# Other columns for the accumulators of a weighted sum, in a kernel that runs a state-space layer and a local attention side by side

## The chip, the cores and the metric

The kernel runs on one core of a Trainium2 chip. The metric is the device time of one execution in microseconds (us). Before the change the median of three executions is 146.32 us (145.62 to 147.16).

## The reference

Two independent layers read two inputs x of 2048 positions by 448 channels (bf16), and their results are laid side by side. Part A is a diagonal complex recurrence with 448 states, part B is attention with 16 heads of 28 channels, in which each position looks at itself and at seven earlier positions, two apart.

```python
# A: h[t] = Lam_bar * h[t-1] + B_bar x[t];  y = 2 Re(C h) + x * Dskip
Bu = jnp.einsum("bld,pd->blp", x + 0j, B_bar)
for t in range(L):
    h = Lam_bar[None, :] * h + Bu[:, t, :]
y = 2.0 * jnp.einsum("blp,dp->bld", hseq, Cmat).real + x * Dskip[None, None, :]
# B: H = 16, Dh = 28, W = 8, dil = 2
qkv = (x @ wqkv) ...            # q, k, v of (H, S, Dh)
idx = pos[:, None] - off[None, :]          # off = 0, 2, ..., 14
logits = jnp.einsum("bhsd,bhswd->bhsw", q, kg) * scale    # kg, vg gathered by idx
attn = _softmax(logits, axis=-1)           # masked where idx < 0
o = jnp.einsum("bhsw,bhswd->bhsd", attn, vg)
out_B = o.reshape(B, S, D) @ wo
return jnp.concatenate([y, out_B], axis=-1)
```

## The kernel before

A position is 16 p + j: the partition p (128 of them) counts blocks of 16 positions, and j (0 to 15) counts inside a block. The neighbours of a position in part B then mostly lie in the same partition at another j; those that fall into the block before are copied there, one partition down. These copies of v are the "halo": its rows 0 to 13 in the tile `vd` stand ahead of the 16 rows of v itself. `halo` (L746) issues two transfers (L749, L750) for each of four groups of rows.

Part B works in this order. TensorE projects q and k (`qk_ps`, L472 to L505) and v (`v_ps`, L735); ScalarE and VectorE evict them from PSUM. VectorE multiplies q and k (L639, L643), TensorE adds the products up by head into `logits` (L654, L660). `softmax` runs for two halves of j, b = 1 (j from 8) and b = 0: a maximum on VectorE (L677, L679), its subtraction on TensorE (L683), the exponential on ScalarE (L689), the sum on TensorE (`sm_ps`, L694), the reciprocal and the product on VectorE (L698, L700), transposes on TensorE (`pt_at`, L706) and a copy by ScalarE (L711). Then `pv` forms the weighted sum of v on VectorE: for each of four groups g = 3, 2, 1, 0 of four rows j, four products of 3584 columns (L791), three additions (L794) and one last addition that folds the two halves of the accumulator (L803; for g = 0 TensorE adds the halves, L806 and L843). The first product of a group is written straight into the accumulator. A DMA transpose (L831) turns the folded accumulators of g = 3, 2, 1 for the last projection (`wo_ps`, L860), ScalarE evicts that (L866) and SyncE's queue sends it out (L869).

Part A multiplies x by B (`scP`, `scb`, L1181 and L1189), runs the recurrence as a scan of doubling steps for seven groups m of states on TensorE (L1198 to L1258) with a ScalarE eviction after each step, and ends with y = C h (`y_ps`, L1345, and the skip term), evicted by ScalarE (L1354) or VectorE (L1356) and sent out by L1359. VectorE also builds the tables of powers `pw` (L1135).

Memory is re-used. The tile `rb` (13568 columns, tag "RB") holds the weights of q and k in columns 0 to 3583, those of v in 3584 to 5375 and x in 5376 to 13567. When q and k are projected, `load_c` loads C over the first weights: eight transfers (L958) into `cn2`, columns 0 to 3583 of `rb`, and one DMA transpose of these (L962) into the tile `Ccat`, which y = C h reads. After that `pv` asks the pool for a second tile with the same tag, `rb2`, which takes the place of `rb`; the accumulators lie in it. In the same way `vd` (tag "RA") takes the place of the tile `ra`, which held the raw x of part B for j from 12 (`x3`, columns 0 to 1855) and the raw B of part A (`bX`, columns 7168 to 10751, read by L1119). `late` (tag "RC") takes the place of q and k. The pool's framework, not the kernel, puts the semaphores in, from the accesses that it sees in program order.

The order of the work is written out by hand. Every piece of work is a unit of a `Planner`, numbered in the order of its `P.add`, with an engine, a cost, dependences and a priority. If `ORDER` has as many entries as there are units (604), as here, the sorted order is replaced by it:

```python
        if len(ORDER) == n:
            for i in ORDER:
                u = self.units[i % 1000]
                u.on = u.eng[i // 1000]
                order.append((0.0, u, 0.0))
            order = order[n:]
        for _, u, _ in order:
            if len(u.eng) > 1:
                u.fn(u.on)
            else:
                u.fn()
```

An entry from 1000 on gives a unit that two engines can do to the second of them (VectorE instead of ScalarE). The units that matter here:

| unit | what | line |
|---|---|---|
| 481, 482, 483, 484 | the four halo groups, SP, two transfers each | L749, L750 |
| 154 | loads of C into `rb`, SP, eight transfers | L958 |
| 155 | transpose of C into `Ccat`, SP | L962 |
| 171, 172 | loads of wo, SP, eight transfers, and their copies to the other partitions, two | L394, L399, L400 |
| 561, 562 | row of Dskip into `rb2`, and x of part A into `late`, SP | L1309, L1318 |
| 485 to 488 | weighted sum of g = 3, VectorE | L791 to L803 |
| 213, 215, 216, 217 | second softmax (b = 0): subtraction, sum, reciprocal with product, transposes | L683, L694, L698, L706 |
| 493, 494, 528 | transposes of the folded accumulators g = 3, 2, 1, SP | L831 |
| 601, 597, 603 | last three outputs of A, SP | L1359 |
| 538, 543, 548, 533 | last four outputs of B (j = 1, 2, 3, 0), SP | L869 |

SP, ScalarE, VectorE, GpSimd and TensorE each run their units in the order of `ORDER`; a unit that waits holds up those behind it on its engine.

Of the kernel before, what the change touches and what calls it, by code (L numbers as in the profile page):

```python
# [10 lines left out]
ALU = mybir.AluOpType  # L11
# [7 lines left out]
NCH = 128  # L19
# [21 lines left out]
FILL = (1, 3)  # L41
PRI = dict(bm=-5.66, xa=2.77, cc=19.9, sc=2.9, ch=-27.35, bk=-0.56, v0=16.0, v1=-26.16, wo=-13.74, y=14.16, pw=-5.68, sm=13.48, lim=100.0, lim2=30.0, limv=70.0, qk=0.86, K11=-14.0, Q11=-13.0, K10=-12.0, Q10=-11.0, K01=-10.0, Q01=-9.0, K00=-8.0, Q00=-7.0, d3=10.94, h0=-1.0, g0=-1.0, h1=-1.0, g1=-1.0, h2=-1.0, g2=-1.0, h3=1.0, g3=-1.0, h4=-1.0, g4=-1.0, h5=-1.0, g5=-1.0, h6=1.0, g6=1.0, nd=4.0, xd=20.12)
ORDER = [
# [28 lines left out]
TWO_PI = 2.0 * math.pi  # L72
MAGIC = 12582912.0

# [234 lines left out]
class PartB:  # L309
# [411 lines left out]
    def v_proj(self, prio, deps):  # L721
        nc, pool, P, cx = self.nc, self.pool, self.plan, self.cx
        self.u_v, self.u_vh, self.u_vm = {}, {}, []

        def va():
            if not hasattr(self, "vd"):
                t = pool.tile([NCH, TJ * D], bf16, name="vd", tag="RA")
                self.vd = t[:].rearrange("p (j d h) -> p j d h", d=DH, h=H)
        for n, j in enumerate((8, 9, 10, 11, 12, 13, 14, 15, 7, 6, 5, 4, 3, 2, 1, 0)):
            box = {}  # L730

            def mm(j=j, box=box):
                ps = box["ps"] = self.psum.tile([NCH, H, DH], f32, name="v_ps", tag="s")
                for k in range(KT):
                    nc.tensor.matmul(ps[:].rearrange("p h d -> p (h d)"), lhsT=self.xT[:, j, k, :],  # L735
                                     rhs=self.wv[:, k, :], start=(k == 0), stop=(k == KT - 1))

            def ev(eng, j=j, box=box):
                va()
                cx.copy(eng, self.vd[:, HALO + j], box["ps"][:].rearrange("p h d -> p d h"))  # L740
            u = P.add("PE", pe(4, 448), mm, [self.u_x[j], self.u_w[2], *deps],
                      prio[n // 8], acq="s")
            self.u_vm.append(u)
            self.u_v[j] = cx.evict(448, ev, [u, *deps], prio[n // 8], rel="s", until=PRI["limv"])

        def halo(i0, i1):  # L746
            f = lambda a, b, p0, p1: self.vd[p0:p1, a:b].rearrange("p j d h -> p (j d h)")
            s0, s1 = i0 + T, i1 + T
            nc.sync.dma_start(f(i0, i1, 1, 113), f(s0, s1, 0, 112))  # L749
            nc.sync.dma_start(f(i0, i1, 113, 128), f(s0, s1, 112, 127))  # L750

        def zero():
            va()
            nc.gpsimd.memset(self.vd[0:1, 0:HALO].rearrange("p j d h -> p (j d h)"), 0.0)
        z = P.add("POOL", 6.0, zero, deps, prio[0])
        for i0, i1 in ((10, 14), (6, 10), (2, 6), (0, 2)):
            h = P.add("SP", 0.2, lambda i0=i0, i1=i1: halo(i0, i1), [self.u_v[i + 2] for i in range(i0, i1)],
                      prio[1], lat=4.0)
            for i in range(i0, i1):
                self.u_vh[i] = [h, z]  # L760

    def pv(self, b, prio, deps):
# [3 lines left out]
        def alloc():  # L766
            if not hasattr(self, "rb2"):
                self.rb2 = pool.tile([NCH, 13568], bf16, name="rb2", tag="RB")
                self.acc = {}
                for i, g in enumerate((3, 2, 1, 0)):  # L770
                    self.acc[g] = self.rb2[:, 1792 * i:1792 * i + 3584]
                self.oT = self.rb2[:, 10752:12288].rearrange("p (r k c) -> p r k c", r=3, k=KT)
                self.oT_ring = Ring(3)
        n1 = 4 * D
        lasts = {}
        for r in (1, 0):
            last = getattr(self, "pv_last", None)
            us = (5, 4, 1, 0)
            for n in range(4):

                def step(n=n, r=r, part=0):
# [13 lines left out]
                    if n == 0:  # L795
                        mul(0)
                        mul(1)
                    elif n < 3:
                        mul(n + 1)
                        add(n)  # L800
                    elif 2 * b + r > 0:
                        add(3)
                        V.tensor_tensor(acc[:, 0:n1], acc[:, 0:n1], acc[:, n1:2 * n1], op=ALU.add)  # L803
                    else:
                        a, t = (v.rearrange("p (y j c) -> p y j c", y=2, j=4)[:, :, 2 * part:2 * part + 2] for v in (acc, tmp[3]))
                        V.tensor_tensor(a, a, t, op=ALU.add)  # L806
# [17 lines left out]
        for r in (1, 0):  # L824
            g = 2 * b + r
            if g > 0:

                def trd(g=g):
                    o = (0, 1792, 0, 8960)[g]
                    t = self.oTd[g] = self.rb2[:, o:o + n1].rearrange("p (k q) -> p k q", q=NCH)  # L830
                    nc.sync.dma_start(t, self.acc[g][:, 0:n1], transpose=True)  # L831
                trs[r] = P.add("SP", 2.5, trd, [lasts[r][1]], PRI["wo"], lat=2.0)
        for j in range(j0, j0 + JB):
            jb = {}
# [2 lines left out]
            def tr(j=j, jb=jb):  # L837
                pt = jb["pt"] = self.psum.tile([NCH, KT, NCH], f32, name="pt_o", tag="s")
                a = j % 4 * D
                for kt in range(KT):  # L840
                    for y in range(2):
                        c = 5376 + y * n1 + a + kt * NCH
                        nc.tensor.matmul(pt[:, kt, :], lhsT=self.rb2[:, c:c + NCH], rhs=cx.ident[:],  # L843
                                         start=(kt == 0 and y == 0), stop=(y == 1), skip_group_check=True)

# [540 lines left out]
def kernel(  # L1386
# [51 lines left out]
    b.softmax(0, 2.6)  # L1438
    a.scan(PRI["sc"], b.u_prod[0] + b.u_prod[1])
    b.v_proj((PRI["v0"], PRI["v1"]), a.u_bm)  # L1440
    b.pv(1, 4, a.u_cc)
    b.pv(0, 5, [])
    a.load_skip([b.u_first])
    a.outputs(PRI["y"])
    plan.run()
# [30 lines left out]
```

## Time and profile before

| | |
|---|---|
| median of three executions | 146.32 us (145.62 to 147.16) |
| the profiled execution | 147.02 us |
| its span, first to last instruction | 145.3 us |
| TensorE busy | 136.7 us (94%) |
| VectorE busy | 122.7 us (84%) |
| ScalarE busy | 91.5 us (63%) |
| mean granted clock of TensorE | 0.986 |
| all DMA traffic | 15.99 MB, mean 110 GB/s |

Times in the views are microseconds from the first instruction. PE is TensorE's matmuls, DVE VectorE, ACT ScalarE, POOL GpSimd, SP SyncE, and SPq its queue of DMA issues. A name like `L791` is a line of the kernel, `rb<-attn,vd` what is written and read; numbers behind tile names are left out, so `rb` also stands for `rb2`. The granted clock is the share of TensorE's full speed that it was given.

### The profile page before, as it was taken

To read this page: it belongs to the slowest core of one execution; us is meant where nothing else is said; L and a number is where in the kernel's file an instruction comes from. 1 tells how busy PE (TensorE), PEld (TensorE's weight loads), DVE (VectorE), ACT (ScalarE), POOL (GpSimd) and SP (SyncE) were. 2 spreads that over 40 slices of the span, in tenths; PEclk is the share of its full clock that TensorE was granted. 3 is DMA by queue.
4 is the path that set the end of the run, shared out by engine and by line. 5 is a ranking of instruction groups with operands and counts; after the bars stand their busy time and mean duration, and the time that the engine had idled before them with its cause. 6 is when DMAs were issued, how large, how long until landed. Compare 5 with 4: busy or idle time off the path is not lost.

```text
span 145.3 us, 2812 instructions
## 1 busy us (share of the span) xinstructions
PE 136.7 (94%) x1078; PEld 72.1 (50%) x1078; DVE 122.7 (84%) x132; ACT 91.5 (63%) x179; POOL 24.8 (17%) x68
## 2 busy tenths in 40 slices
PE   5999999999999999999997599999999999999990
PEld 1633433456464455675363246445565555555660
DVE  3357899999989899893299999999999999999740
ACT  3336969999775964667886239867984434224181
POOL 7382399901920000000000000000000000000000
PEclk9999999999999999999999959999999999999999
DMA  4955434995347448989452000640019252734034
GB/s 132 258 110 106 81 70 82 264 191 62 81 85 71 94 123 176 164 245 196 101 120 58 0 0 5 122 131 0 34 45 162 87 184 82 170 99 145 13 122 131
DMA packets 39390, 15.99 MB, mean 110 GB/s; under 512 B 31445, under 2 KB 38740, under 8 KB 39377
## 3 DMA queue, kind: packets, MB, share of 16 engines
q1 hardware_dynamic: 39314, 15.82, 50.0%
q8 instruction: 8, 0.13, 0.4%
q14 instruction: 5, 0.04, 0.1%
q10 hardware_dynamic: 63, 0.01, 0.0%
HBM read 4.27 MB, written 3.67 MB: 55 GB/s over the span
## 4 chain that ended last, share of the span: by engine, by line
PE 71%; ACT 10%; DVE 7%; DMA 5%; POOL 2%; issue 2%; SPq 1%; POOLq 0%; DVEq 0%; ACTq 0%
PE y_ps L1345 15%; PE wo_ps L860 8%; PE qk_ps L472 7%; PE v_ps L735 7%; DMA Ccat<-rb 5%; PE scb L1181 5%; PE scP L1181 5%; ACT qk L204 3%; ACT qk L202 3%; DVE prods L791 3%; PE logits L654 3%; PE scb L1198 2%; PE y_ps L1342 2%; PE scb L1223 2%; PE qk_ps L479 1%
## 5 line engine op out<-in xcount | busy, mean ns | idle before, releaser
L639 DVE TENSOR_TENSOR prods<-qk 128x3072 bf16<-128x3072 bf16 (+1 forms) x18 | 24.8, 1412 | 1.0 <-PE logits L654 0.6
L791 DVE TENSOR_TENSOR prods<-attn,vd 128x3584 bf16<-128x3584 bf16 x12 | 24.0, 2018 | 0.0
L794 DVE TENSOR_TENSOR rb<-rb,prods 128x3584 bf16<-128x3584 bf16 x11 | 22.2, 2020 | 0.1
L1218 ACT CAST pbuf<-scb 128x128 bf16<-128x128 f32 x35 | 9.3, 279 | 9.0 <-PE scb L1223 7.5
L472 PE MATMUL qk_ps<-rb 128*128 128x512 bf16 x60 | 14.9, 385 | 0.0
L1345 PE MATMUL y_ps<-Ccat,late 128*128 128x448 bf16 x64 | 14.9, 352 | 0.0
L860 PE MATMUL wo_ps<-wo_p,rb 128*128 128x448 bf16 x64 | 13.7, 352 | 0.0
L735 PE MATMUL v_ps<-rb 128*128 128x448 bf16 x64 | 13.3, 353 | 0.0
L1354 ACT CAST late<-y_ps 128x896 bf16<-128x896 f32 x6 | 5.4, 905 | 11.4 <-PE y_ps L1345 11.4
L791 DVE TENSOR_TENSOR rb<-attn,vd 128x3584 bf16<-128x3584 bf16 x4 | 8.1, 2023 | 4.9 <-DMA Ccat<-rb 4.8
L1181 PE MATMUL scb<-xaT_sb,Bcat 128*128 128x512 bf16 x42 | 11.7, 398 | 0.0
L1345 PE MATMUL y_ps<-Ccat,h 128*128 128x448 bf16 x48 | 11.7, 353 | 0.0
L1181 PEld LDWEIGHTS <-Bcat 128*128 128x128 bf16 x84 | 7.6, 99 | 7.8 <-issue 2.4
L1181 PE MATMUL scP<-xaT_sb,Bcat 128*128 128x512 bf16 x42 | 11.2, 379 | 0.0
L202 ACT CAST qk<-qk_ps 128x512 bf16<-128x512 f32 (+2 forms) x13 | 7.4, 582 | 4.7 <-PE qk_ps L472 3.2
L866 ACT CAST late<-wo_ps 128x448 bf16<-128x448 f32 x16 | 8.2, 540 | 3.3 <-PE wo_ps L860 2.8
L202 ACT CAST vd<-v_ps 128x448 bf16<-128x448 f32 x16 | 8.0, 542 | 2.8 <-PE v_ps L735 2.7
L1223 PEld LDWEIGHTS <-pw 128*128 128x128 bf16 x70 | 5.8, 101 | 7.6 <-issue 4.5
L472 PEld LDWEIGHTS <-rb 128*128 128x128 bf16 x60 | 5.8, 100 | 7.1 <-issue 1.2
L1345 PEld LDWEIGHTS <-late 128*128 128x128 bf16 x64 | 6.3, 98 | 5.8
L643 DVE TENSOR_TENSOR prods<-qk 128x768 bf16<-128x768 bf16 (+3 forms) x18 | 9.1, 566 | 0.0
L204 ACT ACTIVATE qk<-qk_ps 128x512 bf16<-128x512 f32 (+1 forms) x15 | 8.5, 603 | 0.2 <-PE qk_ps L505 0.2
(177 smaller groups left out, 256.8 us busy)
## 6 DMA issues: line engine op xcount, KB each, us to landing
out_dram<-late SPq DMA_DIRECT2D x18, 112.0 KB, 1.7
out_dram<-late SPq DMA_DIRECT2D x7, 224.0 KB, 2.3
vd<-vd SPq DMA_DIRECT2D x3, 392.0 KB, 4.2
rb<-in_B_wqkv_dram SPq DMA_DIRECT2D x3, 336.0 KB, 4.5
late<-in_A_x_dram SPq DMA_DIRECT2D x1, 448.0 KB, 4.1
ra<-in_A_B_re_dram SPq DMA_DIRECT2D x1, 392.0 KB, 4.4
ra<-in_A_B_im_dram SPq DMA_DIRECT2D x1, 392.0 KB
rb<-in_A_C_re_dram SPq DMA_DIRECT2D x4, 98.0 KB, 3.0
```

What stands on the lines that cost most here:

```text
L202: nc.scalar.copy(out, in_)
L204: nc.scalar.mul(out, in_, scale)
L472: nc.tensor.matmul(out(n), lhsT=w(n, full, k), rhs=self.xT[:, j:j + 4, k, :], start=(not rfirst and k == 1), stop=(rfirst and k == KT - 1) ...
L639: V.tensor_tensor(out.rearrange("p i j k q -> p i (j k) q"), qq.unsqueeze(1).to_broadcast([NCH, 2, 4 * nk, NCH]), bass.AP(kk.tensor, kk.of ...
L643: V.tensor_tensor(jk(out[:, i, a:e]), qq, kk, op=ALU.mult)
L735: nc.tensor.matmul(ps[:].rearrange("p h d -> p (h d)"), lhsT=self.xT[:, j, k, :], rhs=self.wv[:, k, :], start=(k == 0), stop=(k == KT - 1))
L791: V.tensor_tensor(tmp[i].rearrange("p (j d h) -> p j d h", j=8, d=DH), aa, self.vd[:, o:o + 8], op=ALU.mult)
L794: V.tensor_tensor(acc, acc, tmp[i], op=ALU.add)
L860: nc.tensor.matmul(ps[:], lhsT=o[:, kt, :], rhs=self.wo_p[:, KT * e + kt, :], start=(kt == 0), stop=(kt == KT - 1))
L1181: mt(box[i], lhsT=self.Bcat[:, k, m, :], rhs=self.xk(slice(i, None, 4), k), start=(i % 2 == 0 and k == 0), stop=False, **kw)
L1218: nc.scalar.copy(pb[:, dst, PAD:], box[3][:, 384:512])
L1345: nc.tensor.matmul(ps, lhsT=self.h[m][:, i, g * NCH:(g + 1) * NCH], rhs=self.Ccat[:, m, :], start=(m == 0 and not skip), stop=(m == NM - 1 ...
```

## The change

The accumulators are laid in the other order: g = 3 in columns 5376 to 8959 of `rb2`, g = 2 in 3584 to 7167, g = 1 in 1792 to 5375 and g = 0 in 0 to 3583. Before, g = 3 lay in 0 to 3583 and g = 0 in 5376 to 8959. The fold now writes the upper half of an accumulator, since the next one takes its lower half, and the transposes and the last transposes on TensorE read and write the places that follow from that. As many instructions of the same shapes run as before. The dependence on the transposed C (`a.u_cc`) is given to the `pv` of b = 0 instead of that of b = 1, and the cost of the halo units that the planner reckons with is 1.45 instead of 0.2. `ORDER` is another one, with the same 604 units: many neighbours change places, seven evictions and copies around the projections of q and k change engines (45, 63, 67 and 68 go to ScalarE, 44, 47 and 70 to VectorE), and several transfers change places on SP's queue. The places of `ORDER` that matter, then the rest of the diff:

```diff
...
-    239, 268, 240, 269, 476, 241, 242, 270, 243, 477, 479, 204, 196, 200, 289, 291, 290, 319, 484, 481, 154,
-    483, 482, 155, 171, 172, 212, 480, 244, 271, 245, 292, 272, 246, 247, 248, 273, 249, 274, 250, 251, 252,
...
+    476, 269, 240, 288, 241, 242, 477, 243, 270, 202, 198, 199, 200, 289, 291, 271, 244, 245, 292, 290, 319,
+    483, 482, 484, 481, 154, 171, 155, 172, 212, 480, 272, 246, 247, 273, 248, 249, 274, 250, 252, 251, 293,
...
-    585, 557, 554, 560, 534, 535, 599, 563, 600, 602, 596, 539, 540, 536, 544, 529, 541, 537, 545, 530, 542,
-    546, 547, 601, 597, 538, 603, 548, 543, 383, 416, 382, 415, 447, 446, 531, 532, 533]
...
+    589, 551, 560, 534, 535, 599, 563, 600, 602, 596, 539, 540, 536, 544, 529, 541, 537, 545, 530, 542, 546,
+    547, 543, 538, 601, 597, 603, 548, 383, 382, 415, 416, 446, 531, 532, 533, 447]
...
-            h = P.add("SP", 0.2, lambda i0=i0, i1=i1: halo(i0, i1), [self.u_v[i + 2] for i in range(i0, i1)],
+            h = P.add("SP", 1.45, lambda i0=i0, i1=i1: halo(i0, i1), [self.u_v[i + 2] for i in range(i0, i1)],
...
-                for i, g in enumerate((3, 2, 1, 0)):
-                    self.acc[g] = self.rb2[:, 1792 * i:1792 * i + 3584]
+                for g in range(4):
+                    self.acc[g] = self.rb2[:, 1792 * g:1792 * g + 3584]
...
-                        V.tensor_tensor(acc[:, 0:n1], acc[:, 0:n1], acc[:, n1:2 * n1], op=ALU.add)
+                        V.tensor_tensor(acc[:, n1:2 * n1], acc[:, 0:n1], acc[:, n1:2 * n1], op=ALU.add)
...
-                    o = (0, 1792, 0, 8960)[g]
+                    o = (0, 5376, 7168, 8960)[g]
                     t = self.oTd[g] = self.rb2[:, o:o + n1].rearrange("p (k q) -> p k q", q=NCH)
-                    nc.sync.dma_start(t, self.acc[g][:, 0:n1], transpose=True)
+                    nc.sync.dma_start(t, self.acc[g][:, n1:2 * n1], transpose=True)
...
-                        c = 5376 + y * n1 + a + kt * NCH
+                        c = y * n1 + a + kt * NCH
...
-    b.pv(1, 4, a.u_cc)
-    b.pv(0, 5, [])
+    b.pv(1, 4, [])
+    b.pv(0, 5, a.u_cc)
```

48 rows, old and new, of the table ORDER are left out of this document.

## The prediction, made before the changed kernel was run

> **What bounds the kernel now.** I read the shares of the engines first, then the chain that ended last, then the table of waits, then single engines in order of time. Page, part 1:
> ```profile
> PE 136.7 (94%) x1078; PEld 72.1 (50%) x1078; DVE 122.7 (84%) x132; ACT 91.5 (63%) x179; POOL 24.8 (17%) x68
> ```
> TensorE is busy 136.7 of 145.3 us; 3.8 us before its first transposes and 3.4 us behind its last matmul (141.9) are ends that any version has. So little idle time is left inside, and it matters where it lies. The chain in order of time (start, length, what):
> ```profile
> 62.82 0.83 SPq L750
> ...
> 63.82 7.98 DMA Ccat<-rb
> ...
> 71.88 2.02 DVE rb L791
> ...
> 78.84 1.94 DVE rb L794
> 80.78 0.88 DVE rsum L698
> ...
> 81.70 0.37 PE scb L1189
> ```
> One transfer stands on the path: the transpose of the staged C into Ccat. The waits (who waited for whom: us, times, longest) say who stood still:
> ```profile
> POOL vd L754 <- PE ps_b L1119: 6.5, 1, 6.5
> ...
> DVE rb L791 <- DMA Ccat<-rb: 4.8, 1, 4.8
> ...
> PE scb L1189 <- DVE rsum L698: 2.8, 1, 2.8
> ```
> VectorE waits 4.8 us (67.08 to 71.88) with the first product of the weighted sum. The reciprocal of the second softmax stands behind it in VectorE's order and is late; it holds the PSUM bank that TensorE's L1189 wants, and TensorE stands for 2.8 us (78.91 to 81.70). Behind the gap the granted clock falls (1 us stages; the last three columns are clock, DMA share, GB/s):
> ```profile
> 83.00:84.00 1.00, 1.00 (x6) 0.47 (x5) 1.00 (x2) 0.40 (x2) 0.00 (x0) 0.58 0.00 0
> 84.00:85.00 1.00, 1.00 (x6) 0.62 (x5) 1.00 (x2) 0.00 (x0) 0.00 (x0) 0.50 0.00 0
> 85.00:86.00 1.00, 1.00 (x3) 0.30 (x2) 1.00 (x2) 0.82 (x2) 0.00 (x0) 0.50 0.00 0
> 86.00:87.00 1.00, 1.00 (x6) 0.56 (x5) 1.00 (x1) 0.25 (x3) 0.00 (x0) 0.72 0.00 0
> ```
> That costs 0.42 + 0.50 + 0.50 + 0.28 = 1.7 us. From 87 to 141.9 TensorE is full (4.85 and 4.91 of 5 us in the two stages from 95 to 105, else 5.00). So the end is the landing of Ccat plus a fixed 73.5 us (145.3 - 71.8): what moves the landing moves the end.
>
> **The wait itself, which the change is about.** The new columns take the first accumulator (now 5376 to 8960) off C's (0 to 3584). This helps only if columns decide. The accumulators are in rb2, a second tile with rb's tag, so what counts is what the first write to a re-used place waits for. The kernel has the same situation once more: vd re-uses the place of ra. The zeroing at L754 writes row 0, columns 0 to 6272 of it; L1119 reads columns 7168 to 10752 of ra. They share no byte. What ra holds in the memset's columns is x3 (0 to 1856), last read by transposes that end at 6.1 us. Yet (GpSimd, then TensorE, in order of time):
> ```profile
> 35.62 5.32 POOL L754 MEMSET vd<- 1x6272 bf16 x1 [6.55 <-PE ps_b L1119]
> ...
> 34.89 0.62 PE L1119 MATMUL ps_b<-Gd,ra 128*128 128x128 bf16 x8
> ```
> GpSimd, free since 29.1, waited until 35.62, 0.1 us behind the last of those matmuls (35.51). The units' dependences do not explain it: they only sort, the written ORDER replaces even that, and run() then only calls the functions. So the first write waits for every earlier access to the old tile, whatever its columns. By that row L791 still waits for the transpose, wherever its accumulator lies. Moving `a.u_cc` from one pv call to the other, and the halo's cost 0.2 -> 1.45, are inputs to the sorter alone and cost nothing here.
>
> **What the change moves on SP's queue.** The new ORDER has other places for the transfers ahead of L791. Before, the queue was (issue time, length):
> ```profile
> 57.34 2.79 SPq L958 DMA_DIRECT2D rb<-in_A_C_im_dram  x4
> 60.23 0.59 SPq L749 DMA_DIRECT2D vd<-vd  x1
> ...
> 62.82 0.83 SPq L750 DMA_DIRECT2D vd<-vd  x1
> 63.82 4.46 SPq L962 DMA_TRANSPOSE Ccat<-rb  x1
> 68.34 4.95 SPq L394 DMA_DIRECT2D wo_p<-in_B_wo_dram  x8
> ```
> After: all four halos (eight transfers), the eight loads of C, the eight loads of wo, and only then the transpose. Halos and C stand ahead of it in both orders and take the same issue time; the eight loads of wo are new in front.
> - Start of the transpose: at most 4.95 us later (the row), at least 8 x 0.428 = 3.4 us (the median of the eight; the longest, 1.19 us, seems to have waited for the transpose itself). I take 4.2.
> - From start to landing it took 7.98 us: 4.46 of issue and 3.5 behind it, with the DMA engines over-full (share 1.24 and 1.25 from 67 to 69 us). After, the halos are long through. The nearest shorter tail is that of the x transposes: 2.8 us to landing, 1.26 of it issue, so 1.5. Between 1.5 and 3.5 I take 2.4, since wo's loads (1.9 to 2.9 us to landing) are still under way: 1.1 us won.
> - Landing: + 4.2 - 1.1 = **+3.1 us**, 74.9 instead of 71.8; bounds 3.4 - 2.0 = +1.4 and +4.95.
>
> VectorE's stall becomes 7.9 us. Queued behind it are the rest of the products, two tables of powers and the softmax's reciprocal, for which TensorE waits: its gap goes from 2.8 to 5.9 us, and all behind it moves by 3.1. The wo loads come earlier, but their first reader is at 100.5. The transfer of L1318 is put ahead of the transposes of L831; its reader is at 135.7, so nothing.
>
> **The clock behind the longer gap.** No row shows a 5.9 us gap. It can cost nothing (1.7 us won) or twice as much (1.7 lost); I take no change, since the one gap seen cost 1.7. [...]
>
> **The other moves in ORDER.** Ahead of 67 us single evictions change between ScalarE and VectorE, loads of x and matmuls of v_proj change places. A moved eviction is about 0.6 us (L202, 582 ns), two of them 1.2. They are hidden by VectorE's wait (4.8 us, then 7.9) and TensorE's gap; without that cover they would count in full. Behind the gap TensorE only swaps neighbours; 0, bounds -0.3 and +0.3. At the end SP's order changes. Before:
> ```profile
> 138.25 1.91 SPq L1359 DMA_DIRECT2D out_dram<-late  x2
> 140.26 0.42 SPq L869 DMA_DIRECT2D out_dram<-late  x1
> 140.73 0.45 SPq L1359 DMA_DIRECT2D out_dram<-late  x1
> 141.71 1.30 SPq L869 DMA_DIRECT2D out_dram<-late  x3
> ```
> After, unit 543 (part B's row j=2) comes first; its eviction ends at 140.93 in the clock of before. The other six outputs queue behind it, three of A that went out from 138.25 on among them. Seven issues at 0.45 from 140.97 end at 144.1; before the last ended at 143.0: **+1.0 us**, bounds 0 and +1.1.
>
> **Sum.** 145.3 + 3.1 + 1.0 + 0 = 149.4 us of span. The profiled execution took 147.02, 1.7 around its span, and is 0.7 above the median of the three runs (146.32); the sum of changes, +4.1, goes onto the median: **150.4 us**.
>
> **Rivals.**
> - *Columns decide after all.* Then VectorE starts L791 at 67.1; products, powers and sum bring it to the reciprocal at 76.0 instead of 80.8, the sums it reads are complete at 76.1, the bank is free at 77.1, ahead of TensorE's 78.9. The gap (2.8) and the slow clock (1.7) go, the tail (+1.0) stays: 146.3 - 3.5 = 142.8, faster. For it: C's columns are free of the first accumulator, and the product's other inputs are there (v's last eviction ends at 65.5). Against it: the row of L754. It decides if the first write to rb2 needs no landing of Ccat.
> - *The wait stays, but lands no later*, because wo's loads fit in time that SP otherwise spends waiting. Then only the tail counts: 147.3, no measurable change. Against it: SP's rows from 51.4 to 68.3 leave 0.2 us between issues at most, so nothing is there to fill.
> - *The wait stays and the clock doubles its loss*, with the full 4.95: 146.3 + 4.95 + 1.0 + 1.7 = 154.0. It belongs to the forecast as its upper end.
>
> **How the numbers follow.** Wait stays and lands later: 0.91; columns decide: 0.05; no later: 0.04. A measurement of this kernel tells about 1% from no change. Of the first case 0.01 lies below 1%, so slower 0.90, same 0.05, faster 0.05. The forecast's own ends are 146.3 + 1.4 = 147.7 and 154.0; the range, 147.6 to 153.4, leaves out both rivals below it and the top of the last.
>
> **What would show it.** Right: in the waits L791 behind Ccat with about 8 us instead of 4.8, L1189 behind L698 with about 6, the loads of L394 issued ahead of L962, Ccat landing near 75, and a last SP group of seven outputs. Wrong: no wait of VectorE for Ccat, VectorE full from 67 on; or a transpose that starts within 1 us of 63.8. If the gap is there but the end moves less, the clock row behind it or TensorE's work ahead of it has taken up the difference.

## The result, and the profile after

The changed kernel takes 150.72 us (median of 4 executions, 149.48 to 151.24) against 145.97 us for the kernel before beside it (145.58 to 147.16): a ratio of 1.030, 95% interval 1.021 to 1.039. It is slower, by about what was forecast (150.4). The profiled execution took 150.89 us, with a span of 149.1 us instead of 145.3. Single executions of one kernel differ by some per cent (e9: 145.37 to 149.09 us), so a ratio compares only executions within 1.5% of the fastest of their kernel; e9 and e11 below have only one such execution and get no ratio, and their traces are of slower ones.

Part 1 of the page, after: busy time of each engine, its share of the span, instructions.

```profile
PE 135.9 (91%) x1073; PEld 72.1 (48%) x1078; DVE 122.4 (82%) x131; ACT 92.4 (62%) x180; POOL 25.5 (17%) x68
```

VectorE and TensorE do the same work as before (122.4 against 122.7, 135.9 against 136.7); what is new in the span is waiting. (The weight loads are 1078 as before, so five matmuls are missing from this trace's records. ScalarE has one eviction more and VectorE one less.) The waits of after (who waited for whom: us, times, longest):

```profile
POOL vd L754 <- ACT Bcat L202: 6.8, 1, 6.8
...
DVE rb L791 <- DMA Ccat<-rb: 6.8, 1, 6.8
...
PE scb L1189 <- DVE rsum L698: 4.8, 1, 4.8
```

VectorE still waits for the transpose of C, although the first accumulator no longer lies where C was staged, and it waits 6.8 us instead of 4.8. TensorE's gap at L1189 grows by the same 2 us, from 2.8 to 4.8. The memset of L754 again starts 0.1 us behind the last matmul that reads `ra` (35.87 against 35.76); the view now names a ScalarE eviction of the same moment. The chain that ended last, after (start, length, what):

```profile
67.86 0.42 SPq L394
68.28 0.04 issue
68.32 5.68 DMA Ccat<-rb
...
74.09 2.02 DVE rb L791
...
82.98 0.88 DVE rsum L698
83.86 0.04 issue
83.91 0.58 PE scb L1189
```

Before, the step ahead of the transfer was a halo's issue at 62.82 (L750); now it is the last load of wo. SP's queue of after in order of time:

```profile
57.75 2.69 SPq L958 DMA_DIRECT2D rb<-in_A_C_re_dram  x4
60.49 3.83 SPq L958 DMA_DIRECT2D rb<-in_A_C_im_dram  x4
64.36 3.92 SPq L394 DMA_DIRECT2D wo_p<-in_B_wo_dram  x8
68.32 3.83 SPq L962 DMA_TRANSPOSE Ccat<-rb  x1
```

The transpose starts 4.5 us later (68.32 against 63.82) and takes 5.68 instead of 7.98 us to its landing, so Ccat lands 2.2 us later. From the start of L791 to the end of the span it was 73.42 us (145.3 - 71.88) and is 75.01 (149.1 - 74.09): another 1.6 us. Its larger part is SP's last outputs, of which the last three groups are now (the length of a group includes the waits between its issues):

```profile
135.00 9.32 SPq L869 DMA_DIRECT2D out_dram<-late  x4
144.41 1.43 SPq L1359 DMA_DIRECT2D out_dram<-late  x3
145.93 0.89 SPq L869 DMA_DIRECT2D out_dram<-late  x2
```

Outputs of A that went out from 138.25 on before stand behind the output of unit 543 until 144.41.

### The profile page after: what moved, and what is told of

Read it like the earlier page. It is cut to its first block, busy times and chain, and to the rows that moved or that the text cites. A ratio compares the mean times of both kernels' runs of the same rounds, so it can differ in the third digit from the quotient of the medians.

```text
span 149.1 us, 2804 instructions
## 1 busy us (share of the span) xinstructions
PE 135.9 (91%) x1073; PEld 72.1 (48%) x1078; DVE 122.4 (82%) x131; ACT 92.4 (62%) x180; POOL 25.5 (17%) x68
## 4 chain that ended last, share of the span: by engine, by line
PE 54%; SPq 21%; DVE 11%; DMA 7%; ACT 2%; issue 2%; DVEq 0%
PE y_ps L1345 14%; SPq L354 9%; PE wo_ps L860 8%; PE v_ps L735 7%; DVE prods L639 4%; DMA Ccat<-rb 4%; PE scP L1181 4%; PE scb L1181 4%; SPq L958 3%; DMA dsk_raw<-in_A_Dskip_dram 3%; DVE prods L791 3%; SPq L394 2%; PE scb L1223 2%; SPq L357 2%; PE y_ps L1342 2%
## 5 line engine op out<-in xcount | busy, mean ns | idle before, releaser
L791 DVE TENSOR_TENSOR prods<-attn,vd 128x3584 bf16<-128x3584 bf16 x12 | 24.0, 2017 | 0.0
L1345 PE MATMUL y_ps<-Ccat,late 128*128 128x448 bf16 x64 | 14.9, 352 | 0.0
L791 DVE TENSOR_TENSOR rb<-attn,vd 128x3584 bf16<-128x3584 bf16 x4 | 8.1, 2022 | 6.9 <-DMA Ccat<-rb 6.8
L1181 PE MATMUL scb<-xaT_sb,Bcat 128*128 128x512 bf16 x42 | 12.2, 416 | 0.1
L204 ACT ACTIVATE qk<-qk_ps 128x512 bf16<-128x512 f32 (+1 forms) x17 | 9.6, 597 | 3.1 <-PE qk_ps L479 2.7
L1194 ACT CAST eP<-scP 128x1024 bf16<-128x1024 f32 x7 | 7.1, 1015 | 2.9 <-PE scP L1189 2.9
```

What stands on the lines that cost most here:

```text
L204: nc.scalar.mul(out, in_, scale)
L791: V.tensor_tensor(tmp[i].rearrange("p (j d h) -> p j d h", j=8, d=DH), aa, self.vd[:, o:o + 8], op=ALU.mult)
L1181: mt(box[i], lhsT=self.Bcat[:, k, m, :], rhs=self.xk(slice(i, None, 4), k), start=(i % 2 == 0 and k == 0), stop=False, **kw)
L1345: nc.tensor.matmul(ps, lhsT=self.h[m][:, i, g * NCH:(g + 1) * NCH], rhs=self.Ccat[:, m, :], start=(m == 0 and not skip), stop=(m == NM - 1 ...
```

## The experiments

All times of one group below come from one chip; the kernel before ran beside each group.

### The columns and the order, each alone

e1 takes the new columns (and the halo's cost and `a.u_cc`) with the old `ORDER`; e2 the old columns with the new `ORDER`.

> The new columns with the old ORDER. Theory 1 (the first write to the re-used place waits for every access to the old tile, so columns don't matter): as before, 146.0 us (145.0 to 147.0); in the waits VectorE's L791 behind Ccat 4.8 us (4.3 to 5.3), TensorE's L1189 behind L698 2.8 us, Ccat landing at 71.8. Rival (columns decide, and the new ORDER made up for it): no such wait, VectorE starts L791 at 67.1, about 141.5 us (146.0 - 2.8 - 1.7).

> The old columns with the new ORDER. Theory 1 (ORDER alone makes the slowdown, by the transpose of C behind the loads of wo and by the last outputs): as after, 150.7 us (149.4 to 151.9), L791 behind Ccat 6.8 us, L1189 behind L698 4.8 us, last output issue 2.4 us behind ScalarE's last eviction start. Rival (the new columns cost something of their own, such as the fold into the upper half): between 146.0 and 149.5 us.

Measured beside a before of 145.38 us: e1 145.92, ratio 1.008 (1.002 to 1.014); e2 150.47, ratio 1.037 (1.025 to 1.049). The order is the loss; the columns alone win nothing. Waits of e1:

```profile
DVE rb L791 <- DMA Ccat<-rb: 4.7, 1, 4.7
PE scb L1189 <- DVE rsum L698: 2.7, 1, 2.7
```

They are nearly those of the kernel before (4.8 and 2.8). The 0.8% of e1 are under the 1% by which executions of before differ (145.58 to 147.16 us beside the changed kernel); its trace shows no place for them (span 144.3, and 73.46 us from the first product to the end, against 73.42 before).

### Is it the tile that VectorE waits for?

e5, e6 and e7 write the accumulators into the old tile instead of a second one with its tag: e5 in the changed kernel, e6 in e1, e7 in the kernel before. e8 is e5 with the old order of the last outputs.

```diff
-        self.rb2 = pool.tile([NCH, 13568], bf16, name="rb2", tag="RB")
+        self.rb2 = self.rb
```

> The changed kernel with one line more: rb2 is not a second tile in the place of rb but rb itself, so that accesses are compared by columns inside one tile. Theory 1 (the re-use of the place made the wait): no wait of VectorE for Ccat although the transpose still lands near 74; L791 starts near 67.4, the reciprocal near 76.3, TensorE's gap of 4.8 us and the half clock (2.1 us) behind it go; the longer tail (1.2 us) stays: 146.0 - 2.8 - 1.7 + 1.2 = 142.7 us (141.5 to 144.0). Rival (something else holds L791, such as the halos or the last projection of v): a wait of some us stays under another name, 145 us or more.

> New columns, old ORDER, and rb2 is rb itself. Theory 1: as the run before but without the longer tail: 146.0 - 2.8 - 1.7 = 141.5 us (140.4 to 142.8), no gap of TensorE near 79. Rival (the gap of TensorE had a second cause that takes its place, such as the power table or the sums of the softmax): a gap of 1 us or more near 79 and 143 us or more.

> The kernel before with rb2 being rb itself: old columns, old ORDER. Theory 1 (then columns decide, and the old columns 0 to 3583 are C's): the wait for Ccat stays at 4.8 us and the time at 146.0 us (145.0 to 147.0). Rival (one tile instead of two is itself faster, whatever the columns): 144 us or less, no wait.

Measured beside a before of 146.94 us: e5 143.67, ratio 0.978 (0.970 to 0.985); e6 142.64, ratio 0.969 (0.961 to 0.976); e7 146.44, ratio 0.999 (0.996 to 1.002). The wait of e7:

```profile
DVE rb L791 <- DMA Ccat<-rb: 4.4, 1, 4.4
```

In e5 and e6 there is no such line; L791 starts at 66.73 and 66.92, although the transpose is issued only at 67.97 in e5. VectorE in e5 (start, length, ..., idle before and its releaser):

```profile
66.73 2.02 DVE L791 TENSOR_TENSOR rb<-attn,vd 128x3584 bf16<-128x3584 bf16 x1
...
75.92 0.96 DVE L698 RECIPROCAL rsum<-sm_ps 128x128 f32<-128x128 f32 x1 [0.30 <-PE sm_ps L694]
```

So both are needed: columns that are free, and one tile. With one tile the wait goes by columns: it stays with the old columns (e7) and goes with the new ones (e5, e6). With a second tile on the same place the columns don't count (e1). That is the first step of the prediction, tested by its opposite. The reciprocal of e5, at 75.92 behind a wait of 0.30, is also where the first rival of the prediction had put it (76.0).

### The outputs at the end

```diff
-    547, 543, 538, 601, 597, 603, 548, ...
+    547, 601, 597, 538, 603, 548, 543, ...
```

> The changed kernel with the last outputs on SP in the old order (601, 597, 538, 603, 548, 543, 533). Theory 1 (issue on SP is the end): everything to ScalarE's last eviction as in the changed kernel, the last issue about 1.2 us earlier, 149.5 us (148.3 to 150.7). Rival (the outputs' landing or their traffic is the end, the order doesn't matter): 150.7 us.

> The changed kernel with rb2 being rb itself and the last outputs in the old order. Theory 1 (the three causes add up): 142.7 - 1.2 = 141.5 us (140.4 to 142.8), as with the old ORDER. Rival (the new ORDER loses somewhere else too): 1 us or more above the run with the old ORDER.

e4, the changed kernel with this edit, has the ratio 1.028 (1.014 to 1.042). Three of its executions took 147.78 to 149.88 us; the profiled one took 352 us, so there is no trace to compare. By the ratios it is 1.3 us below e2, which has the outputs in the new order and the old columns, but the two intervals overlap. e8 decides: 142.45 us, ratio 0.968 (0.962 to 0.974), with every execution (142.19 to 142.70) below every one of e5 (143.56 to 144.08), and 1.2 us lower by the medians. The order of the outputs costs 1.2 us. e8 is also level with e6 (142.64), so with one tile the rest of the new `ORDER` costs nothing.

### What delays the transpose?

The prediction blamed the loads of wo alone. e3 puts the transpose back ahead of them in the changed kernel.

```diff
-    483, 482, 484, 481, 154, 171, 155, 172, ...
+    483, 482, 484, 481, 154, 155, 171, 172, ...
```

> The changed kernel with units 155 and 171 exchanged in ORDER: the transpose of C ahead of the loads of wo. Theory 1: it is issued at 64.4 instead of 68.3 and lands 5.7 to 8.0 us later, at 70.1 to 72.4 instead of 74.0, so VectorE's wait is 2.9 to 5.2 us instead of 6.8 and the end 1.6 to 3.9 us earlier plus up to 0.4 of clock: 148.0 us (146.5 to 149.2). Rival (the landing is set by traffic of the halos and of C, not by the place in the queue): landing at 73.5 or later, 150.0 us or more.

Measured 149.39 us (148.97 to 149.85), ratio 1.033 (1.022 to 1.044), in the group of e1 and e2. That is above the range I had given (up to 149.2), and VectorE still waits 5.9 us. SP's queue of e3, then SP's waits:

```profile
59.75 3.48 SPq L958 DMA_DIRECT2D rb<-in_A_C_im_dram  x4
65.44 3.71 SPq L962 DMA_TRANSPOSE Ccat<-rb  x1
```

```profile
SPq L962 <- DMA rb<-in_A_C_im_dram: 2.0, 3, 1.1
```

The last load of C is issued by 63.23 and the transpose starts at 65.44: it stands 2.2 us until C has landed. In the old order the issues of two halo groups (60.23 to 63.65 in the trace of before) lay in that time. The new order moves C's loads behind all four halos, and the prediction had costed this at nothing ("Halos and C stand ahead of it in both orders and take the same issue time"). The last group takes the two moves apart; e9 undoes both, e10 leaves only wo in front, e11 is e9 with the old outputs too, e12 is the changed kernel again:

```diff
-    483, 482, 484, 481, 154, 171, 155, 172, ...
+    484, 481, 154, 483, 482, 155, 171, 172, ...   # e9, e11
+    484, 481, 154, 483, 482, 171, 155, 172, ...   # e10
```

> After, with C's loads, the last two halos, the transpose of C and the loads of wo back in the order that SP had before; the columns, the order of all other work and of the outputs stay new. My theory now: two moves on SP's queue make the longer wait together, C's loads behind all halos (the transpose then has to wait for C's last load) and wo's loads ahead of the transpose; both are undone here. So L791 waits for Ccat about 4.8 us again (4.3 to 5.3), L1189 about 2.8, and only the tail's 1.2 us is left: 1.2 above the kernel before beside it, ratio 1.008, 147.4 us where before is 146.2. Rival: something else in the new order (evictions, loads of x, v_proj) feeds the wait; then it stays near 6 us and the time near 149.5.

> After, with C's loads back ahead of the last two halos, but wo's eight loads still ahead of the transpose of C. Theory 1: SP issues without a pause in either case, so the transpose starts at the same time as in the changed kernel (about 68.2 us) and by then C has landed in both: L791 waits 6.2 to 6.8 us, time as after, ratio 1.030, 150.5 us where before is 146.2. Theory 2: the two moves add up, each with its own share (the run with the transpose ahead of wo had a wait of 5.9 us, the changed kernel 6.8): then the wait is 5.7 us and the time 1.1 us below after, about 149.4. The prediction's own working (start 4.2 later, 1.1 won behind it, with no help from C's place) would have a wait of 7.9 us and 150.4.

> As the run with SP's old places ahead of the transpose, and the last outputs in the old order too; the new columns and the rest of the new order stay. Theory: SP's queue is the whole loss, so this is the kernel before again: ratio 1.000 (0.996 to 1.006), 146.2 us where before is 146.2, wait 4.8 us. Rival: the moves among TensorE, VectorE and ScalarE cost something of their own; then 0.5 us or more above before.

> The changed kernel itself, on the chip of the three others, so that they can be compared with it: ratio 1.030 (1.021 to 1.039), 150.6 us where before is 146.2; L791 waits 6.8 us for Ccat, L1189 4.75 us.

Measured beside a before of 146.84 us: e9 147.94 (lowest 145.37), e10 150.37 (ratio 1.036, 1.000 to 1.071), e11 146.36 (lowest 143.92, where the lowest of before is 143.96), e12 150.25 (ratio 1.037, 1.026 to 1.048). One row for each trace; "half clock" is the time at 0.50 behind the gap, summed from 1 us stages, "rest" the span from the start of the first L791 on (the spans are rounded to 0.1 us, so it is good to 0.05):

| kernel | SP ahead of the transpose | wait of L791 | start to landing | half clock | outputs | rest |
|---|---|---|---|---|---|---|
| before | old | 4.80 | 7.98 | 3.4 | old | 73.42 |
| e1 | old | 4.71 | 7.76 | 3.4 | old | 73.46 |
| e7 | old | 4.45 | 7.42 | 3.4 | old | 73.45 |
| e11 | old | 4.22 | - | 0 | old | 73.40 |
| e9 | old | 5.26 | 8.23 | 0 | new | 74.69 |
| e3 | C late | 5.90 | 7.27 | 3.4 | new | 74.71 |
| e10 | wo in front | 5.92 | 6.18 | 6.8 | new | 75.40 |
| e2 | both | 6.13 | 6.27 | 3.4 | new | 74.64 |
| e12 | both | 6.40 | 6.58 | 3.4 | new | 74.71 |
| after | both | 6.76 | 5.68 | 6.8 | new | 75.01 |

(In e11 the trace puts the wait on the exponential on ScalarE (L689) that ended at the same moment, and lists no landing.)

With SP's old places the wait is 4.7 on average over five traces, with the new ones 6.4 over three: 1.7 us from the queue alone, with the columns old (e2) or new. Each move alone gives 1.2 (e3, e10), each read from one trace, while traces with the same queue differ by up to 1.0 (4.22 to 5.26). The queue itself is steadier: from the issue of its first halo to the start of the transpose it takes 12.4 to 13.2 us with the old places, 14.9 in e3, 16.1 in e10, and 16.5 to 17.1 with both moves. So the two together, 4.1 on average, are less than their sum, 2.1 + 3.3: the issue of wo's loads (3.9 us in e10 and after) covers the time in which C lands (2.2 us of standing in e3). For e10 neither of my two theories is settled: its wait, 5.9, is nearer to 5.7 than to 6.2, its time is that of e12. The 7.9 that the prediction's own working would give is refuted. The moves among TensorE, VectorE and ScalarE cost nothing that can be told: e11, which keeps all of them, is no slower than before.

## Why the prediction was right

Its sum was 3.1 + 1.0 + 0 = 4.1. The two profiled spans differ by 3.8: 2.21 in the start of the first product, 1.26 in the outputs (rest of the traces with the new outputs and at most 3.4 us of half clock, 74.69 on average, less the 73.43 of the old), 0.32 behind the longer gap. (The medians differ by 4.75, since the profiled execution of before was 1 us above its median.) That the sum came so near is in part luck: the landing was over-sized by 0.9, and the outputs and the clock were under-sized by 0.3 each.

- **The wait stays.** Right, and shown: e1 against e6, e7 against e6. What decided was the row of L754, a wait of the same kind at another place of the same trace.
- **Start of the transpose, +4.2.** Measured +4.5, and +4.1 on average from the first halo on. Right in size, but 1.2 us of wait are there without wo's loads (e3): the step that passed over the place of C's loads failed, and it did not show because wo's loads cover them. So the second rival, that wo's loads fit into time in which SP would wait, was true of about 2.2 of their 3.9 us; the prediction had looked for such time in the queue of before, where the halos fill it.
- **From start to landing, 1.1 won.** Under-sized: 2.3 in after, and 1.6 on average between the four traces with wo in front (5.68 to 6.58) and the five with wo behind (7.27 to 8.23). The reason given was the halos. They are long through in e3 too, and it takes 7.27; it is wo's place that decides. Why loads of wo behind the transpose make its landing later was not tested.
- **Landing and gap.** +2.2 instead of +3.1, and so 4.75 instead of 5.9 us of gap.
- **The clock, 0 with +-1.7.** In after TensorE is slow longer (stage, engines, then clock, DMA share, GB/s):

```profile
83.00:84.00 1.00, 0.10 (x1) 0.00 (x0) 0.90 (x2) 0.00 (x0) 0.00 (x0) 0.50 0.00 0
...
87.00:88.00 1.00, 1.00 (x4) 0.39 (x3) 1.00 (x1) 0.69 (x2) 0.00 (x0) 0.50 0.00 0
88.00:89.00 1.00, 0.95 (x9) 0.65 (x9) 1.00 (x2) 0.53 (x2) 0.00 (x0) 0.91 0.00 0
```

- From 83.91 to the return of full clock at 88.2 that is 4.3 us at half clock, 2.1 lost instead of 1.7. Taking no change was about right, but the lower bound, 1.7 won, was not to be had. The last columns of the table say that no half clock (e9, e11) and 3.4 us of it give the same rest, so the loss of 1.7 was not on the path: where TensorE loses nothing there, it waits later. The times agree: 3.4 us at half clock take 1.2% off the mean clock of an execution, and in the group of e5 to e8 two executions of before with a mean of 1.00 took 146.88 and 146.96 us, beside 145.45 to 146.94 for those with 0.988. Waits of e9:

```profile
PEld L860 <- DVE prods L791: 1.0, 1, 1.0
...
PE wo_ps L860 <- DVE prods L791: 0.5, 1, 0.5
```

- Behind the landing VectorE's products are as long a path as TensorE's work, and what goes beyond one slow stretch seems to count: 0.3 in after, 0.7 in e10 (one trace each). VectorE's last additions of the weighted sum, in before and then in after:

```profile
133.73 2.09 DVE L806 TENSOR_TENSOR rb<-rb,prods 128x1792 bf16<-128x1792 bf16 x2
```

```profile
135.92 2.09 DVE L806 TENSOR_TENSOR rb<-rb,prods 128x1792 bf16<-128x1792 bf16 x2
```

- From the start of the first L791 to the end of these it is 63.9 us in both (71.88 to 135.82, 74.09 to 138.01), and also in e9, e10 and e11, whatever the clock did; none of the five traces lists another wait of VectorE in that stretch. So a later landing moves the end through VectorE itself, and not only, as the prediction had it, through the reciprocal and TensorE's gap. (Single executions of before were as low as 143.4 us at a clock of 1.00; no trace shows what comes earlier in them, and that stays open.)
- **The outputs, +1.0.** Measured 1.26, and 1.2 from e8 against e5 (the prediction's own seven issues, up to 144.1 instead of 143.0, give 1.1).
- **"Fixed 73.5 us" behind the landing.** It held (73.40 to 73.46 in four traces with the old outputs), and not because TensorE is full alone: VectorE is full too, and TensorE has room for 1.7 us of lost clock.
- **Rival "columns decide", 142.8.** Refuted as a course of this change, but its number was good: e5, which makes it true, has the ratio 0.978, or 143.0 on the 146.32 of before. Its 4.5 us (gap and slow clock of TensorE) came out because VectorE's wait, which goes too, is nearly as long, 4.8: the slow clock alone, as shown above, wins nothing.

e6 and e8 beat both kernels, 3.1% and 3.2% below before: the new columns in one and the same tile.

## What to carry to other kernels

Where a tile re-uses the place of another, look in the trace of before for a first write of that kind and what it waited for; here it waited for all of the old tile, and moving columns inside the new one won nothing (e1, ratio 1.008) until both were one tile (e6, 0.969). Look at what stands on a queue between a load and the transfer that reads it: in e3, with nothing between, the transpose stood 2.2 us until C had landed. Ask also what could stand behind a transfer that the path waits for: in e10 loads of wo that are read only from 100.5 us on (in the trace of before) were issued ahead of it and made its start 3.3 us later. Before a stretch at a lower clock is counted as a loss, ask whether a second engine is as long on the path; here none of it (e9) and 3.4 us of it (e12) left the same rest, 74.69 and 74.71 us.

## What the runs showed of the hardware

Half clock at the gap lasted 3.4 us in six of the ten traces of the table (83.16 to 86.57 before, 83.96 to 87.38 in e12), 6.8 us in two (81.36 to 88.18 after, 80.74 to 87.58 in e10), and it did not come in the other two. The length of the gap alone does not tell which: there was none in e9 behind a gap of 3.25 us, longer than the 2.79 of before. Nor did it begin at one distance from the gap: before, TensorE had been back for 1.46 us (81.70 to 83.16), and after, it was to stand for another 2.55 us (81.36 to 83.91). What decides whether and when half clock comes was not shown. Behind the gap it cost TensorE 1.7 us before and in e12, and 2.1 after.

The transpose of C kept SP's queue for 3.7 (e3) to 4.9 us (e9) in these traces, and its landing came 5.7 (after) to 8.2 us (e9) after its start. Eight loads of wo took 3.9 us of SP ahead of it (e2, e10, e12, after) and 4.8 (e3) to 5.3 (e7) behind it.
